# The first head pair's k in a top-32 attention with two gated MLPs: its low parts on VectorE, its last 64 rows first

## The chip, the cores and the metric

One Trainium2 chip, one of its cores. TensorE (PE in the profile; PEld is its weight load) multiplies, VectorE (DVE), ScalarE (ACT) and GpSimd (POOL) do the rest, SyncE (SP) issues the DMAs. The metric is the device time of one execution in microseconds, as the median of three runs: 790.08 us (789.1 to 790.63).

## The reference

For two batches of eight heads, 576 rows and 64 columns, attention keeps for each row the 32 largest scores; two MLPs follow on the 1152 rows of 512.

```
scores = scale * q @ k^T
kth    = the 32nd largest score of each row
attn   = exp(scores - max) where scores >= kth, else 0; divided by its sum
x      = attn @ v, heads side by side          # 1152 x 512
h      = x @ w_in ; g = h * tanh(softplus(h)) ; x = g @ w_out
out    = ((x @ w_a) * (x @ w_b)) @ w_out2
```

The inputs are random float32 values. The MLP weights come as float64 bits and are converted on the chip.

## The kernel before

**Tiles.** The 1152 rows of q make nine tiles of 128 (t = 0 to 8; tile J = 4 holds the last 64 rows of both batches). For each tile there are four steps, one for each pair of heads (hp = 0 to 3). A step transposes and scales q (`prep_q`), and in tiles 0 and 4 also prepares the pair's k (`prep_k`, L106 to L128, for batch 0 and batch 1). Then TensorE makes the scores in four pieces of 288 columns (L176), and ScalarE copies each from PSUM to the tile s2 (L178). VectorE searches the 32 largest: four rounds of MAX8 (L192) with three of MATCH_REPLACE8 (L195) between, for both heads (`largest`). `weighted_sum` (L205) makes the exponentials, transposes them (L227) and multiplies by v (L234).

**High and low parts.** Products that decide which scores are largest are made of two parts: a rounded high part (a cast on ScalarE) and a low part, the remainder (a subtraction). In `prep_k`, `km` holds both parts of the first 512 rows of k for two heads and `kn` those of the last 64 rows. L116 casts, L117 subtracts. The engine of the subtraction comes from `KSUB = (0, 1)`: GpSimd in batch 0, VectorE in batch 1. TensorE then transposes `km` (L122) and `kn` (L125), head by head, and ScalarE copies the results into `kks` (L127), the operand of the scores.

**Weights.** `convert_` (L283) takes 68 tiles of 128x512 from float64 to float32: L293, L294 and L297 on ScalarE, L295 on VectorE, L298 and L299 on GpSimd. It loads them at L288 and stores the result at L306. `weight_` loads them again (L325) and splits them where wanted (L332 to L335).

**MLPs.** Three blocks of tiles (0 to 2, 3 to 5, 6 to 8) go through `gated` and `bilinear`. `product` is L362, `add_product` L369. In `gated` the chain for one slice of columns is: min (L404) on VectorE, four activations on ScalarE, a product (L409) on VectorE, then `gate_parts` (L376, L377), which casts gh on ScalarE and subtracts gl on GpSimd or VectorE. At a block's end y is copied (L417), transposed (L351) and split into yh (ScalarE, L344) and yl (VectorE, L346); `bilinear` multiplies both.

**What sets the order.** Attention and MLP work is written as streams that `together` interleaves. A scheduler then lists the instructions of each engine by priority and by the times that it assumes; each engine works through its list in order. So a small change near the start can move instructions far behind it. PSUM tiles named bank have three buffers, and ks, kr, km and kn have one each.

Of the kernel before, what the change touches and what calls it, by code (L numbers as in the profile page):

```python
# [9 lines left out]
F32 = mybir.dt.float32  # L10
# [22 lines left out]
KSUB = (0, 1)  # L33
# [18 lines left out]
def topk_attention_mlps(ctx: ExitStack, tc: tile.TileContext, q, k, v, w, out):  # L52
# [6 lines left out]
    nc = tc.nc  # L59
    B, H, S, D = q.shape  # L60
# [5 lines left out]
    SM = J * P  # L66
# [21 lines left out]
    def bank(name, n=512):  # L88
        return ps.tile([P, n], F32, name=name, tag="bank", padded_shape=[P, 512])
# [16 lines left out]
    def prep_k(b, hp):  # L106
        ks = wp.tile([P, 2, J, D], F32, name="ks", bufs=BUFS[4])
        kr = wp.tile([R, 2, D], F32, name="kr", bufs=BUFS[4])
        for s in range(2):
            nc.sync.dma_start(ks[:, s], k[b, 2 * hp + s, 0:SM, :].rearrange("(p j) d -> p j d", j=J))  # L110
        nc.sync.dma_start(kr, k[b, 2 * hp:2 * hp + 2, SM:S, :].rearrange("h p d -> p h d"))
        km = wp.tile([P, 2, J, 2, D], F32R, name="km", bufs=BUFS[4])
        kn = wp.tile([R, 2, 2, D], F32R, name="kn", bufs=BUFS[4])
        for z, raw in ((km, ks), (kn, kr)):
            high, low = (z[..., i, :] for i in range(2))
            nc.scalar.copy(high, raw)  # L116
            (nc.gpsimd, nc.vector)[KSUB[b]].tensor_sub(low, raw, high.bitcast(F32))  # L117
        for s in range(2):
            kk = kks[:, (b * H + 2 * hp + s) % (H + 2), :]
            pk = bank("pk")  # L120
            for j in range(J):
                nc.tensor.transpose(pk[:, j * P:(j + 1) * P], km[:, s, j].rearrange("p z d -> p (z d)").bitcast(F32),  # L122
                                    ident)
            pr = bank("pr", R)
            nc.tensor.transpose(pr, kn[:, s].rearrange("p z d -> p (z d)").bitcast(F32), ident[:R, :R])  # L125
            for src, o, n in ((pk, s * R, SM), (pr, SM * (1 - s), R)):
                nc.scalar.copy(kk[:, o:o + n], src)  # L127
            KK[b, 2 * hp + s] = kk  # L128
# [34 lines left out]
    def scores_(t, hp):  # L163
        if hp == 0:
            load_q(t)
        made = prep_q(t, hp)
        if t in (0, J):
            prep_k(t // J, hp)
        s2 = att.tile([P, 2, S], F32, name="s2", bufs=ABUF[0])
        for s in range(2):  # L170
            h = 2 * hp + s
            parts = [(qq, KK[b, h]) for b, qh, ql in made for qq in (qh, ql)]
            for a in range(2):
                psc = bank("psc", HS)
                for n, (qq, kk) in enumerate(parts):
                    nc.tensor.matmul(psc, qq[:, s, :], kk[:, a * HS:(a + 1) * HS],  # L176
                                     start=(n == 0), stop=(n == len(parts) - 1))
                nc.scalar.copy(s2[:, s, a * HS:(a + 1) * HS], psc)  # L178
        return s2
# [338 lines left out]
```

## Time and profile before

| | |
|---|---|
| median of three runs | 790.08 us |
| the profiled execution | 790.78 us |
| its span, first to last instruction | 789.0 us |
| PE busy | 690.1 us (87%) |
| DVE busy | 571.1 us (72%) |
| ACT busy | 550.8 us (70%) |
| POOL busy | 466.0 us (59%) |

The profile comes from one execution. Busy shares over the span mix stages that have different limits, so the work is read stage by stage. 1.78 us of the profiled execution lie outside the span. Starts are counted from the span's start; an idle time in brackets stands behind the instruction that it came before, with what ended it.

### The profile page before, as it was taken

The numbers are of one execution on the slowest core, as the hardware profiler recorded it, in microseconds if no ns is written. First come the engines' busy times: TensorE is split into PE (matmuls) and PEld (weight loads), VectorE is DVE, ScalarE is ACT, GpSimd is POOL, SyncE is SP. The second block draws the span as 40 slices with busy tenths as digits, with TensorE's granted clock in tenths as the row PEclk, the third lists the DMA queues.
The fourth block names the chain that finished last, engine by engine and source line by source line (L and its number), as shares of the span: only waits on it lengthen the run. The fifth ranks groups of instructions, "written<-read, shape, count | busy, mean of one in ns | idle before, by whom it ended". The sixth has DMA issues, their size and how long they took to land. (4 is left out here: it accounts for less than half of the span.)

```text
span 789.0 us, 12393 instructions
## 1 busy us (share of the span) xinstructions
PE 690.1 (87%) x3988; PEld 572.0 (72%) x3988; DVE 571.1 (72%) x1152; ACT 550.8 (70%) x1262; POOL 466.0 (59%) x390
## 2 busy tenths in 40 slices
PE   3565657789977988999999999988999999989997
PEld 2444535556664757889897888867979999969996
DVE  3999999976798789986679998998601276523331
ACT  5889888888997996666668998976524275553232
POOL 6756566676775751456554465552648767665661
PEclk9987667799997998999999999997999999999999
DMA  8987665889989973134334234221403454433411
GB/s 244 288 272 251 209 204 182 225 256 304 354 282 325 342 232 111 54 95 133 94 90 129 78 90 112 80 68 55 134 15 108 119 173 125 131 105 107 125 51 40
DMA packets 79537, 126.12 MB, mean 160 GB/s; under 512 B 27504, under 2 KB 31600, under 8 KB 79472
## 3 DMA queue, kind: packets, MB, share of 16 engines
q1 hardware_dynamic: 79472, 125.33, 52.3%
q8 instruction: 31, 0.51, 0.3%
q14 instruction: 34, 0.28, 0.1%
HBM read 105.12 MB, written 20.19 MB: 159 GB/s over the span
## 5 line engine op out<-in xcount | busy, mean ns | idle before, releaser
L335 POOL TENSOR_TENSOR whl<-raw,whl 128x512 fp32r<-128x512 f32 x164 | 215.3, 1321 | 161.5 <-ACT whl L334 126.6
L192 DVE MAX8 m<-wk 128x8 f32<-128x576 f32 x216 | 158.5, 749 | 1.1
L362 PE MATMUL ph<-yh,whl 128*128 128x384 f32 x576 | 154.6, 340 | 0.7 <-ACT yh L344 0.7
L298 POOL TENSOR_TENSOR w<-w,w 128x512 int32<-128x512 int32 x68 | 89.0, 1309 | 77.8 <-DVE w L295 40.5
L362 PEld LDWEIGHTS ph<-yh,whl 128*128 128x128 f32 x576 | 105.6, 190 | 4.0 <-ACT yh L344 1.6
L195 DVE MATCH_REPLACE8 wk<-m,wk 128x576 f32<-128x576 f32 x144 | 106.4, 741 | 0.0
L362 PE MATMUL ph<-yl,whl 128*128 128x384 f32 x288 | 98.4, 342 | 0.1
L299 POOL TENSOR_TENSOR w<-w,w 128x512 f32<-128x512 f32 x68 | 89.7, 1322 | 7.0 <-ACT w L297 2.2
L234 PE MATMUL px<-et,v 128*64 128x128 f32 (+1 forms) x800 | 76.6, 297 | 17.3 <-ACT et L228 17.0
L334 ACT CAST whl<-raw 128x512 fp32r<-128x512 f32 x113 | 69.3, 622 | 28.8 <-PE ph L362 16.2
L234 PEld LDWEIGHTS px<-et,v 128*64 128x64 f32 x800 | 53.1, 151 | 40.1 <-ACT et L228 26.8
L377 POOL TENSOR_TENSOR gl<-m,gh 128x384 fp32r<-128x384 f32 x52 | 55.5, 1067 | 42.9 <-ACT gh L376 12.1
L362 PE MATMUL ph<-xh,whl 128*128 128x384 f32 x256 | 71.6, 340 | 0.7 <-DVE m L409 0.7
L192 DVE MAX8 m<-s 128x8 f32<-128x576 f32 x72 | 53.9, 751 | 25.2 <-ACT s L178 24.7
L176 PE MATMUL psc<-kks,qh 128*128 128x288 f32 x160 | 57.2, 377 | 13.8 <-ACT kks L127 7.9
L434 DVE TENSOR_TENSOR m<-ph,e 128x384 f32<-128x384 f32 x36 | 19.9, 554 | 67.9 <-PE ph L362 54.9
L376 ACT CAST gh<-m 128x384 fp32r<-128x384 f32 x68 | 34.8, 511 | 48.8 <-DVE m L434 27.6
L227 PE MATMUL pe<-ident,e 128*128 128x128 f32 x324 | 55.7, 305 | 14.7 <-ACT e L220 7.4
L176 PE MATMUL psc<-kks,ql 128*128 128x288 f32 x160 | 51.4, 352 | 11.5 <-DVE ql L155 11.2
L178 ACT COPY s<-psc 128x288 f32<-128x288 f32 x144 | 52.0, 402 | 13.2 <-PE psc L176 12.4
L293 ACT ACTIVATE w<-w 128x512 f32<-128x512 f32 x68 | 46.5, 684 | 20.3 <-DMA w<-in_w_dram 13.5
L228 ACT COPY et<-pe 128x384 f32<-128x384 f32 x108 | 50.3, 487 | 14.6 <-PE pe L227 14.5
(90 smaller groups left out, 1520.3 us busy)
## 6 DMA issues: line engine op xcount, KB each, us to landing
raw<-ws SPq DMA_DIRECT2D x229, 256.0 KB, 2.8
w<-in_w_dram SPq DMA_DIRECT2D x68, 512.0 KB, 4.8
ws<-w SPq DMA_DIRECT2D x68, 256.0 KB, 4.5
qr<-in_q_dram SPq DMA_DIRECT2D x16, 256.0 KB, 4.2
ks<-in_k_dram SPq DMA_DIRECT2D x16, 128.0 KB, 4.3
v<-in_v_dram SPq DMA_DIRECT2D x16, 128.0 KB, 3.9
out_dram<-o SPq DMA_DIRECT2D x8, 256.0 KB, 3.0
qr<-in_q_dram SPq DMA_DIRECT2D x4, 128.0 KB, 8.1
```

What stands on the lines that cost most here:

```text
L176: nc.tensor.matmul(psc, qq[:, s, :], kk[:, a * HS:(a + 1) * HS], start=(n == 0), stop=(n == len(parts) - 1))
L178: nc.scalar.copy(s2[:, s, a * HS:(a + 1) * HS], psc)
L192: nc.vector.max(m8[:, s, got], src[:, s, :])
L195: nc.vector.match_replace(wk[:, s, :], m8[:, s, got], src[:, s, :], NEG)
L227: nc.tensor.transpose(pe[:, i, :], ef[:, n * P:(n + 1) * P], ident)
L234: nc.tensor.matmul(px[s * D:(s + 1) * D, o:o + n], vt[b][:, 2 * hp + s, j, :] if j < J else v4[b][:, hp, s, :], et[:, i if j < J else J, o ...
L298: nc.gpsimd.tensor_tensor(wi, wi, count, op=ALU.add)
L299: nc.gpsimd.tensor_mul(wf, wf, highf)
L334: nc.scalar.copy(wh, raw)
L335: sub().tensor_sub(wl, raw, wh.bitcast(F32))
L362: nc.tensor.matmul(ph, a, x, start=(i == 0), stop=(i == len(mm) - 1))
L377: sub().tensor_sub(gl, g, gh.bitcast(F32))
```

## The change

In `prep_k` the load of `kr` (the last 64 rows of k) is issued ahead of the two loads of `ks`, and the pair (`kn`, `kr`) is cast and subtracted ahead of (`km`, `ks`). This holds for all eight head pairs. For hp = 0 the subtraction is given to VectorE whatever `KSUB` says; since `KSUB` names VectorE for batch 1 already, that moves two instructions, both in batch 0.

```diff
     def prep_k(b, hp):
         ks = wp.tile([P, 2, J, D], F32, name="ks", bufs=BUFS[4])
         kr = wp.tile([R, 2, D], F32, name="kr", bufs=BUFS[4])
+        nc.sync.dma_start(kr, k[b, 2 * hp:2 * hp + 2, SM:S, :].rearrange("h p d -> p h d"))
         for s in range(2):
             nc.sync.dma_start(ks[:, s], k[b, 2 * hp + s, 0:SM, :].rearrange("(p j) d -> p j d", j=J))
-        nc.sync.dma_start(kr, k[b, 2 * hp:2 * hp + 2, SM:S, :].rearrange("h p d -> p h d"))
         km = wp.tile([P, 2, J, 2, D], F32R, name="km", bufs=BUFS[4])
         kn = wp.tile([R, 2, 2, D], F32R, name="kn", bufs=BUFS[4])
-        for z, raw in ((km, ks), (kn, kr)):
+        for z, raw in ((kn, kr), (km, ks)):
             high, low = (z[..., i, :] for i in range(2))
             nc.scalar.copy(high, raw)
-            (nc.gpsimd, nc.vector)[KSUB[b]].tensor_sub(low, raw, high.bitcast(F32))
+            (nc.vector if hp == 0 else (nc.gpsimd, nc.vector)[KSUB[b]]).tensor_sub(low, raw, high.bitcast(F32))
```

The scheduler's lists change from there on, up to about where attention ends. ScalarE's list near the start, as a piece of the difference (- before, + now); s2_132 is the first pair's tile of scores, km_161 and kn_162 belong to the second pair:

```order
+L178 COPY s2_132<-psc_133 128x288
+L116 CAST kn_162<-kr_157 64x2x64
+L178 COPY s2_132<-psc_137 128x288
 L297 ACTIVATE w64_295<-w64_295 128x512
-L178 COPY s2_132<-psc_133 128x288
+L178 COPY s2_132<-psc_141 128x288
 L116 CAST km_161<-ks_156 128x8x64
-L178 COPY s2_132<-psc_137 128x288
-L178 COPY s2_132<-psc_141 128x288
-L116 CAST kn_162<-kr_157 64x2x64
 L178 COPY s2_132<-psc_145 128x288
```

The first two copies of scores now stand ahead of one activation of the weight conversion, and the first pair's kn cast, which is not in this piece, moved to the head of the list, ahead of the scaling of q.

TensorE's list where block 1 ends (tiles 3 to 5), before; pq and psc are the scores of tile 8, third pair, and gh_5793 and gl_5794 are the parts of the last slice of `gated`:

```order
L369 MATMUL acc<-whl,gh_5793 128x512 x6
L234 MATMUL px<-et,v_2954 64x128 x5
L234 MATMUL px<-et,v_2955 64x128 x2
L144 MATMUL pq<-ident,qr 128x128 x2
L369 MATMUL acc<-whl,gl_5794 128x512 x3
L176 MATMUL psc<-kks,qh 128x288 x2
L176 MATMUL psc<-kks,ql 128x288 x2
L176 MATMUL psc<-kks,qh 128x288
L176 MATMUL psc<-kks,ql 128x288
L176 MATMUL psc<-kks,qh 128x288
L176 MATMUL psc<-kks,ql 128x288
L351 MATMUL pt<-ident,y 128x128 x12
```

And the same place now (gh_5612 and gh_5688 are two slices before the last):

```order
L144 MATMUL pq<-ident,qr 128x128 x2
L369 MATMUL acc<-whl,gh_5612 128x512 x6
L369 MATMUL acc<-whl,gl_5613 128x512 x3
L176 MATMUL psc<-kks,qh 128x288
L369 MATMUL acc<-whl,gh_5688 128x512 x6
L176 MATMUL psc<-kks,qh 128x288
L176 MATMUL psc<-kks,ql 128x288 x2
L176 MATMUL psc<-kks,qh 128x288
L176 MATMUL psc<-kks,ql 128x288
L369 MATMUL acc<-whl,gl_5689 128x512 x3
L176 MATMUL psc<-kks,qh 128x288
L176 MATMUL psc<-kks,ql 128x288
```

Between the transposes of q and the scores' second half there now stand products of the MLP; the last slice's (gh_5793, gl_5794) follow the piece shown, straight ahead of the transposes of y.

VectorE's list at the same block end, before; 6301 is the search of tile 8, third pair, and yl_4529 the low part of block 1's y:

```order
L192 MAX m_6301<-s_5817 128x8 x2
L195 MATCH_REPLACE wk<-m_6301,s_5817 128x576 x2
L346 TENSOR_TENSOR yl_4529<-pt,yh_4528 128x4x128
L192 MAX m_6301<-wk 128x8 x2
L346 TENSOR_TENSOR yl_4529<-pt,yh_4528 128x4x128
L195 MATCH_REPLACE wk<-m_6301,wk 128x576
L346 TENSOR_TENSOR yl_4529<-pt,yh_4528 128x4x128
```

And now:

```order
L192 MAX m_6301<-s_5817 128x8
L195 MATCH_REPLACE wk<-m_6301,s_5817 128x576 x2
L192 MAX m_6301<-wk 128x8 x2
L195 MATCH_REPLACE wk<-m_6301,wk 128x576 x2
L192 MAX m_6301<-wk 128x8
L346 TENSOR_TENSOR yl_4529<-pt,yh_4528 128x4x128
L192 MAX m_6301<-wk 128x8
L195 MATCH_REPLACE wk<-m_6301,wk 128x576
L346 TENSOR_TENSOR yl_4529<-pt,yh_4528 128x4x128 x2
```

More of the search stands ahead of the first and of the third yl than before.

## Rows read from the trace of the kernel before

**Rows 1.** Stretches: PE, PEld, DVE, ACT, POOL busy; then clock, DMA share, GB/s.

```profile
0.00:16.22 16.22, 6.50 (x22) 4.41 (x22) 3.85 (x6) 9.93 (x21) 8.68 (x15) 1.00 0.83 238
25.00:150.00 125.00, 78.78 (x422) 58.49 (x420) 123.02 (x262) 107.05 (x255) 80.61 (x63) 0.77 0.74 227
150.00:312.50 162.50, 140.57 (x779) 99.16 (x777) 131.98 (x268) 144.87 (x323) 102.56 (x93) 0.91 0.86 280
412.00:525.00 113.00, 109.87 (x707) 92.67 (x705) 108.29 (x227) 100.05 (x250) 61.89 (x52) 1.00 0.34 94
525.00:541.00 16.00, 11.48 (x73) 8.52 (x71) 15.83 (x34) 11.61 (x29) 4.99 (x4) 0.75 0.17 50
575.00:789.00 214.00, 205.39 (x1070) 184.40 (x1068) 77.38 (x135) 86.81 (x170) 129.33 (x102) 0.99 0.35 101
```

**Rows 2.** The waits view, TensorE, 0 to 25 us: total, times, longest.

```profile
PE pk L122 <- POOL km L117: 5.7, 2, 3.4
...
PE pr L125 <- POOL kn L117: 1.8, 1, 1.8
```

**Rows 3.** The timeline of the first pair: start, us, engine, line, operation, idle before.

```profile
1.85 1.52 SPq L110 DMA_DIRECT2D ks<-in_k_dram  x2
...
3.88 0.75 SPq L111 DMA_DIRECT2D kr<-in_k_dram  x1
...
7.09 1.26 POOL L117 TENSOR_TENSOR km<-ks,km 128x512 fp32r<-128x512 f32 x1 [4.89 <-ACT km L116]
...
8.27 0.67 ACT L293 ACTIVATE w<-w 128x512 f32<-128x512 f32 x1 [1.27 <-DMA w<-in_w_dram]
...
10.84 0.45 POOL L117 TENSOR_TENSOR kn<-kr,kn 64x128 fp32r<-64x128 f32 x1
...
14.41 0.67 ACT L297 ACTIVATE w<-w 128x512 f32<-128x512 f32 x1
...
14.98 0.38 ACT L178 COPY s<-psc 128x288 f32<-128x288 f32 x1
...
15.26 0.62 ACT L116 CAST km<-ks 128x512 fp32r<-128x512 f32 x1
...
15.78 0.70 ACT L178 COPY s<-psc 128x288 f32<-128x288 f32 x2
...
16.22 1.54 DVE L192 MAX8 m<-s 128x8 f32<-128x576 f32 x2 [1.67 <-ACT s L178]
...
16.56 0.40 ACT L178 COPY s<-psc 128x288 f32<-128x288 f32 x1
```

**Rows 4.** All of VectorE's L117: count, ns min/median/max, first and last start.

```profile
L117 DVE TENSOR_TENSOR km<-ks,km x4: 681/822/1235, 54.6 to 301.9; 128x512 fp32r<-128x512 f32 x4
L117 DVE TENSOR_TENSOR kn<-kr,kn x4: 233/270/280, 55.5 to 303.4; 64x128 fp32r<-64x128 f32 x4
```

**Rows 5.** The timeline where a subtraction on VectorE meets GpSimd.

```profile
268.43 1.29 POOL L299 TENSOR_TENSOR w<-w,w 128x512 f32<-128x512 f32 x1
...
269.03 1.24 DVE L117 TENSOR_TENSOR km<-ks,km 128x512 fp32r<-128x512 f32 x1 [1.38 <-PE acc L369]
```

**Rows 6.** The timeline at the end of block 1.

```profile
519.58 0.54 DVE L404 TENSOR_SCALAR e<-ph 128x384 f32<-128x384 f32 x1
...
527.04 1.65 PE L369 MATMUL acc<-whl,gh 128*128 128x512 f32 x6
...
529.83 0.95 PE L369 MATMUL acc<-whl,gl 128*128 128x512 f32 x3
...
530.39 1.41 DVE L192 MAX8 m<-wk 128x8 f32<-128x576 f32 x2
...
533.85 0.85 PE L176 MATMUL psc<-kks,ql 128*128 128x288 f32 x2 [2.77 <-DVE ql L155]
...
538.25 0.68 DVE L346 TENSOR_TENSOR yl<-pt,yh 128x512 fp32r<-128x512 f32 x1
...
541.50 0.68 DVE L346 TENSOR_TENSOR yl<-pt,yh 128x512 fp32r<-128x512 f32 x1
```

## Prediction

> **What bounds the kernel now.** I read the busy time by stretch first, since no engine bounds the whole span [rows 1]. Up to 16.22 us no search runs: VectorE is busy for 3.85 us of it, and its list waits for the first scores. From 25 to 150 us VectorE is busy for 123.02 of 125 us, so the search of the 32 largest sets the pace and everything else fits beside it. From 150 to 312.5 us nothing is full: ScalarE 144.87, TensorE 140.57, VectorE 131.98 of 162.5 us, with the DMA engines at 0.86. From 412 to 525 us TensorE (109.87 of 113) and VectorE (108.29) are both nearly full. From 525 to 541 us VectorE is full (15.83 of 16) and TensorE, with 11.48 us, waits for it. After 575 us TensorE is nearly full to the end. What moves VectorE's start therefore has a way to the end: the search moves, the MLPs start earlier, and TensorE's idle time shrinks. Where two engines are nearly full, only the order of their lists decides what is left of it.
>
> Then I read the waits of the first 25 us. TensorE waits 5.7 us in two waits for km and 1.8 us in one for kn, both from GpSimd [rows 2]. The timeline of the first pair shows why kn is late: its subtraction starts at 10.84 us, behind the weight conversion in GpSimd's list, while km's started at 7.09 us [rows 3]. It also shows who ends last: the first MAX8 starts at 16.22 us, released by ScalarE's copies of the scores, not by k [rows 3].
>
> **The change part by part.** *Two subtractions leave GpSimd and come to VectorE.* Only the first pair of batch 0 moves; the other hp = 0 case was on VectorE already. GpSimd loses 1.26 + 0.45 = 1.7 us [rows 3]. VectorE gains two instructions of kinds that it already runs four times each, 0.68 to 1.24 us for km and 0.23 to 0.28 us for kn [rows 4]. They fall into the first 16.22 us, where VectorE has over 12 us free [rows 1], so they cost nothing on the path; without that cover they would cost 0.9 to 1.5 us. For the duration I take 0.68 us: the long case at 269.03 us ran while GpSimd's L299 was running from 268.43 us [rows 5], and once km's subtraction has left GpSimd, that list has nothing to do there until w's conversion.
>
> The Trainium skill says of this in "SBUF — State Buffer", section "SBUF: two separate sides", that VectorE and GpSimd share one pair of ports, that an operation of VectorE with two SBUF inputs and one of GpSimd that reads SBUF exclude each other, and that the loser blocks for the whole instruction. The trace agrees: 1.24 us beside GpSimd against a minimum of 0.68 us [rows 4, 5]. By that rule a collision here would add 0.56 us to km's low part; without one nothing is added, and neither is seen in the sum, for the reason that follows.
>
> *kr goes ahead of ks.* The issue of kr takes 0.75 us [rows 3]. It now stands ahead of the two issues of ks and of the first load of w, so these leave up to 0.75 us later, and everything behind them leaves as before. With that, VectorE's km subtraction starts between 7.1 us (GpSimd's start before) and 7.85 us and ends between 7.8 and 9.1 us, against 7.09 + 1.26 = 8.35 us before. So km itself gains little or loses a little. What is gained is kn: it is ready before km, and TensorE's 1.8 us of waiting for it goes [rows 2].
>
> *What is late next is ScalarE's list.* From 8.27 us on, when the first weights land, it works through conversions and copies almost without a pause until the scores come [rows 3]. TensorE's 1.8 us are mostly hidden behind it. So I count in ScalarE's list. Two things leave the part ahead of the first copy of scores: the kn cast, 0.2 us of the list, which moves to its head (two copies of 0.28 us and one such cast lie between 15.78 and 16.56 us, so 0.78 - 0.56), and one conversion, which starts at 14.41 us and holds the list until 14.98 us, 0.57 us [rows 3]. The first copy comes at 14.98 - 0.57 - 0.2 = 14.2 us. The second follows after a copy (14.98 to 15.26 us, 0.28) and a kn cast (0.2), where a copy and a km cast stood (0.80): 14.7 us, done at 15.1 us. The first MAX8 so starts at 15.1 us, 1.1 us earlier. The second head's scores gain only the 0.2 us, since the same conversion and km cast now stand in between: the last copy starts at 16.56 - 0.2 = 16.4 us and is done at 16.8 us. VectorE does one MATCH_REPLACE8 in between, and its three operations are done at 16.8 + 0.7 = 17.5 us. Before, the two MAX8 ended at 16.22 + 1.54 = 17.76 us and a third operation of about 0.7 us ended at 18.4 us. The search is then 0.9 us ahead.
>
> The bounds of this: if the first weights land the full 0.75 us later, ScalarE starts its run that much later, and 0.1 us is left. At most it is the 1.8 us that TensorE waited for kn. I take 0.9 us, because kr is only 32 KB in front of 256 KB of ks and 512 KB of weights: what the weights wait for is the transfers, which go on from 2 us, more than the issue. For the second pair, GpSimd's 1.7 us come out of its list ahead of that pair's km, so its scores come earlier by more than the 0.9 us and the search isn't held up. In pairs 1 to 3 of batch 0 and in batch 1 the order of kr and ks alone changes; VectorE is full there [rows 1], and it costs nothing as long as the scores come as early as now.
>
> *The lists are sorted anew.* This is the unknown, because it reaches from 25 us to about 580 us. I weigh it at the one place where TensorE visibly waits for VectorE between 412 and 575 us. Before, TensorE ends block 1 with all MLP products done and then waits 2.77 us for the low part of q before tile 8's scores [rows 6]; from 525 to 541 us it idles 16 - 11.48 = 4.5 us [rows 1]. Now products of two earlier slices stand among these scores and cover that wait. But the last slice's products come straight ahead of y's transposes, and their own chain is long. From L404 at 519.58 us to the product with gh at 527.04 us it took 7.5 us, and to that with gl at 529.83 us 10.25 us [rows 6]. After the last ph, TensorE's list now has two slices of 9 products, 8 score products and the rest of one px. Six products with gh at 1.65 us and three with gl at 0.95 us are 2.6 us a slice as the rows print them [rows 6], less where they overlap; two slices and some 1.5 us for the rest make 5 to 6.7 us of cover. So TensorE waits 0.8 to 2.5 us for gh, and then for gl, which came 2.8 us after gh while the six gh products take 1.65 us, another 1.1 us. Together 1.9 to 3.6 us: about the 2.8 us removed. One wait takes the place of the other, and I put this term at 0. Its ends are -4.5 us (TensorE's idle time there goes altogether) and +2.8 us (below).
>
> *Sum.* 790.78 us for the profiled execution, -0.9 for the start, 0 for the new order: 789.9 us. The profiled execution is 0.7 us above the median of the runs shown, 790.08 us; against that median the forecast is **789.2 us**.
>
> **The rivals.** *A, the forecast:* 0.9 us earlier, the new order about even; by the bounds at the start and a us of disorder, 787.6 to 790.8 us.
>
> *B, the new order fills TensorE's gap.* For it speaks that TensorE and VectorE are both at 96% or more from 412 to 525 us, so that better mixing pays directly, and that at half speed the clock also suffers from the gap: 0.75 granted from 525 to 541 us [rows 1]. Against it speaks the chain of the last slice. If the chain is covered, 790.08 - 0.9 - 4.5 = 784.7 us.
>
> *C, slower: VectorE reaches block 1's yl later.* Its list now has eleven operations of tile 8's third pair ahead of the third yl where there were seven. Four of them at 0.7 us (two took 1.41 us) are 2.8 us [rows 6]. TensorE's yl products need all three yl. VectorE is full up to there [rows 1], so the four can't hide unless it loses idle time elsewhere: 113 - 108.29 = 4.7 us of it lie between 412 and 525 us [rows 1]. The point from which it decides: if the new order recovers less than 1.9 us of that (2.8 - 0.9), the kernel is slower. With none recovered the third yl moves from 541.5 us [rows 6] by 2.8 - 0.9 = 1.9 us, and the time is 790.08 + 1.9 = 792.0 us, or 792.8 us if the start gives only 0.1.
>
> *D, the change at the start does nothing:* ScalarE's list and the landing of the weights hide it all, or the mixed stretch from 150 to 312.5 us swallows it behind the DMA engines (0.86 busy) and ScalarE. 790.1 us. For it speaks that the first MAX8 was released by ScalarE; against it, that two items really leave ScalarE's list ahead of the scores.
>
> **How the numbers follow.** A 0.38, B 0.25, C 0.26, D 0.11. A measurement of this kernel tells about 0.2% from no change, which is 1.6 us: faster is below 788.5 us, slower above 791.7 us. A spans the first bound: 0.13 faster, 0.25 the same. B is faster; C is slower. D gives 0.09 the same and 0.01 to each side. Together 0.39 faster, 0.34 the same, 0.27 slower. The range goes from B's 784.7 us to C's upper end with a little beyond it, 784.6 to 793.0 us.
>
> **What would show it.** In the profile of the changed kernel: kn's subtraction done before km's, both on VectorE before 9.2 us; no wait of TensorE's L125 for GpSimd; the first MAX8 near 15.1 us and the third operation of the search done near 17.5 us; VectorE about 0.9 us ahead through 150 us; the third yl between 538 and 543 us; TensorE's idle time from 525 to 541 us now in front of the last products or gone. It would be wrong if the first weights land 0.75 us later, so that the first MAX8 starts after 15.8 us, or if the stretch from 150 to 412 us, which I count as unchanged though its lists change too, gains or loses more than a few us of idle time.

## The result and the profile after

| | median | runs | ratio to the kernel before (95%) |
|---|---|---|---|
| before | 790.36 us | 4 | |
| changed | 795.52 us | 4 | 1.0068 [1.0045, 1.0092] |

The change makes the kernel about 5 us slower. The forecast was 789.2 us, 784.6 to 793.0, so the time lies outside the range. The profiled span went from 789.0 to 795.3 us.

The head of the kernel came out as worked out. The timeline of the changed kernel's first pair, to be held against [rows 3] (start, us, engine, line, operation, idle time before and its releaser):

```profile
1.85 0.99 SPq L109 DMA_DIRECT2D kr<-in_k_dram  x1
2.88 1.06 SPq L111 DMA_DIRECT2D ks<-in_k_dram  x2
...
5.96 0.28 DVE L117 TENSOR_TENSOR kn<-kr,kn 64x128 fp32r<-64x128 f32 x1 [5.09 <-ACT kn L116]
7.05 0.69 DVE L117 TENSOR_TENSOR km<-ks,km 128x512 fp32r<-128x512 f32 x1
7.80 1.11 PE L122 MATMUL pk<-ident,km 128*128 128x128 f32 x4 [1.71 <-DVE km L117]
8.41 0.67 ACT L293 ACTIVATE w<-w 128x512 f32<-128x512 f32 x1 [1.40 <-DMA w<-in_w_dram]
8.84 0.37 PE L125 MATMUL pr<-ident,kn 64*128 64x64 f32 x1
...
15.01 0.76 DVE L192 MAX8 m<-s 128x8 f32<-128x576 f32 x1 [0.60 <-ACT s L178]
16.67 0.76 DVE L192 MAX8 m<-s 128x8 f32<-128x576 f32 x1
```

Both subtractions are on VectorE and done at 7.74 us, kn's first; the first weights are converted from 8.41 us instead of 8.27; L125 no longer waits for kn; the first MAX8 starts at 15.01 us (forecast 15.1, before 16.22) and the third operation of the search ends at 16.67 + 0.76 = 17.43 us (forecast 17.5).

The loss shows in the stretches, the same as in [rows 1] (PE, PEld, DVE, ACT, POOL busy; clock, DMA share, GB/s), of the changed kernel:

```profile
25.00:150.00 125.00, 79.69 (x418) 59.76 (x417) 123.94 (x264) 108.98 (x257) 81.11 (x63) 0.75 0.73 227
150.00:312.50 162.50, 134.62 (x706) 93.73 (x707) 124.74 (x247) 137.18 (x300) 101.36 (x89) 0.90 0.87 278
...
525.00:541.00 16.00, 15.08 (x101) 12.37 (x99) 16.00 (x34) 14.45 (x36) 11.41 (x10) 1.00 0.25 67
```

Between 150 and 312.5 us VectorE does 124.74 us of work where it did 131.98, ScalarE 137.18 for 144.87 and TensorE 134.62 for 140.57, while DMA share and GB/s are as before. So each of the three has 6 to 8 us of work less behind it by 312.5 us, and the rate of the transfers is the same, 278 for 280 GB/s.

A milestone narrows it: x of tile 2 (L250). It is the attention result times prs, the reciprocals of the rows' sums, and the tile's MLP starts from it. It stood at 227.86 us before; in the changed kernel it is 8.5 us later:

```profile
236.33 0.66 DVE L250 TENSOR_TENSOR x<-xr,prs 128x512 f32<-128x512 f32 x1
```

The way there shows first at the search of tile 2's last (fourth) pair of heads. VectorE's timeline of the kernel before; the MAX8 opens the search of that pair's first head:

```profile
159.89 0.74 DVE L192 MAX8 m<-s 128x8 f32<-128x576 f32 x1
160.56 0.43 DVE L295 TENSOR_SCALAR w<-w 128x512 int32<-128x512 int32 x1
...
163.78 0.43 DVE L295 TENSOR_SCALAR w<-w 128x512 int32<-128x512 int32 x1
...
166.92 0.41 DVE L295 TENSOR_SCALAR w<-w 128x512 int32<-128x512 int32 x1
```

and of the changed kernel:

```profile
161.16 0.69 DVE L409 SCALAR_TENSOR_TENSOR m<-m,ph 128x512 f32<-128x512 f32 x1 [1.95 <-ACT m L408]
163.25 0.43 DVE L295 TENSOR_SCALAR w<-w 128x512 int32<-128x512 int32 x1 [1.40 <-ACT w L293]
166.70 0.43 DVE L295 TENSOR_SCALAR w<-w 128x512 int32<-128x512 int32 x1 [3.02 <-ACT w L293]
...
167.79 0.76 DVE L192 MAX8 m<-s 128x8 f32<-128x576 f32 x1
```

The weight conversions (L295) come at about the same times, 163.25 for 163.78 and 166.70 for 166.92 us. But this search, which ran between them before, now stands behind two of them in VectorE's list and starts 7.9 us later, while VectorE idles 1.95, 1.40 and 3.02 us. VectorE's list is not the whole cause, for the scores themselves come later. TensorE makes them and ScalarE copies them (L178), before:

```profile
153.53 0.61 PE L176 MATMUL psc<-kks,qh 128*128 128x288 f32 x1 [0.62 <-ACT qh L154]
...
158.94 1.01 ACT L178 COPY s<-psc 128x288 f32<-128x288 f32 x3
```

and in the changed kernel:

```profile
156.35 4.45 PE L369 MATMUL acc<-w,m 128*128 128x512 f32 x8
160.64 2.75 PE L362 MATMUL ph<-xf,raw 128*128 128x256 f32 x12
163.05 0.48 PE L176 MATMUL psc<-kks,qh 128*128 128x288 f32 x1
...
165.93 0.68 ACT L293 ACTIVATE w<-w 128x512 f32<-128x512 f32 x1 [0.83 <-DMA w<-in_w_dram]
...
167.07 0.99 ACT L178 COPY s<-psc 128x288 f32<-128x288 f32 x3
```

TensorE starts these scores 9.5 us later, behind 20 products of the MLP that followed them before, and ScalarE copies them behind one more conversion that waited for its load. So the order of three engines' lists holds this search back.

The waits of VectorE from 140 to 236 us say the same. In front of conversions it idles 15.0 us before and 15.2 in the changed kernel. What grew is its idle time in front of other work, from 3.1 to 8.5 us (total, times, longest), before:

```profile
DVE m L192 <- ACT s L178: 2.1, 2, 1.4
...
DVE e L212 <- ACT e L198: 0.5, 1, 0.5
DVE m L409 <- ACT m L408: 0.5, 1, 0.5
```

and in the changed kernel:

```profile
DVE m L409 <- ACT m L408: 2.5, 3, 2.0
DVE rs L243 <- ACT e L220: 2.4, 1, 2.4
DVE e L212 <- ACT e L198: 2.3, 1, 2.3
...
DVE m L192 <- ACT s L178: 1.3, 3, 0.5
```

All of these are waits for ScalarE, which has the conversions' other steps in its own list.

### The profile page after: what moved, and what is told of

Same layout as the page of the kernel before. It is cut to its first block, busy times and chain, and to the rows that moved or that the text cites. A ratio compares the mean times of both kernels' runs of the same rounds, so it can differ in the third digit from the quotient of the medians.

```text
span 795.3 us, 12384 instructions
## 1 busy us (share of the span) xinstructions
PE 689.4 (87%) x3988; PEld 572.7 (72%) x3988; DVE 572.4 (72%) x1154; ACT 552.8 (70%) x1262; POOL 465.8 (59%) x388
## 5 line engine op out<-in xcount | busy, mean ns | idle before, releaser
L299 POOL TENSOR_TENSOR w<-w,w 128x512 f32<-128x512 f32 x68 | 91.1, 1341 | 7.8 <-ACT w L297 3.5
L234 PEld LDWEIGHTS px<-et,v 128*64 128x64 f32 x800 | 54.8, 154 | 40.2 <-ACT et L228 27.0
L176 PE MATMUL psc<-kks,qh 128*128 128x288 f32 x160 | 55.4, 369 | 16.9 <-ACT qh L154 8.7
L227 PE MATMUL pe<-ident,e 128*128 128x128 f32 x324 | 53.7, 299 | 14.9 <-ACT e L220 9.0
L178 ACT COPY s<-psc 128x288 f32<-128x288 f32 x144 | 52.3, 401 | 10.2 <-PE psc L176 9.1
L369 PE MATMUL po<-whl,gh 128*128 128x512 f32 x216 | 59.4, 397 | 0.0
```

What stands on the lines that cost most here:

```text
L227: nc.tensor.transpose(pe[:, i, :], ef[:, n * P:(n + 1) * P], ident)
L234: nc.tensor.matmul(px[s * D:(s + 1) * D, o:o + n], vt[b][:, 2 * hp + s, j, :] if j < J else v4[b][:, hp, s, :], et[:, i if j < J else J, o ...
L299: nc.gpsimd.tensor_mul(wf, wf, highf)
L369: nc.tensor.matmul(acc[i], z[:, i * P:(i + 1) * P], a, start=(first and m == 0), stop=(last and m == len(mm) - 1))
```

## The experiments

**The theories.** *List theory:* the edits gain about 1 us at the head, and the lists that the scheduler sorted anew lose it and more between 140 and 236 us, where the search shares VectorE's in-order list with conversions that wait for weights. *Edit theory:* the subtractions on VectorE or the other load order cost the time themselves. *Any-order theory:* each other order costs some us, spread over the program.

To tell them apart I pinned each engine's list. Every pinned kernel has this at the end of the kernel function, which only fixes the order within an engine and adds no instruction; LISTS holds five lists, one for each engine:

```diff
+    real = [i for i in nc.cur_bb.bb.instructions if type(i).__name__ not in ("BassTilePoolBoundary", "InstRegisterMove")]
+    after = mybir.DependencyInfo(mybir.DependencyClass.NoSync, mybir.DependencyReason.DATA)
+    for seq in listed():
+        for a, b in zip(seq, seq[1:]):
+            tc.add_manual_dep(real[b], real[a].name, after, reason="order")
```

**The edits without the new lists, and the new lists without the edits.** head18 is the changed code; its LISTS are its own up to 18 us and from there those of the kernel before. tail25 is the code before; its LISTS are its own up to 25 us and from there those of the changed kernel.

> The changed code with both edits, but each engine's list pinned: the changed kernel's own order for what starts before 18 us of its profile, and from there the order that the kernel before had. List theory (the loss is made by the re-sorted lists between 140 and 236 us, and the edits gain about 1 us at the head): 788 to 790 us beside about 790.3 of before, 0.9 to 2 us faster at best; prs of tile 2 back at about 221 to 223 us. Edit theory (the two edits themselves cost the time, by two subtractions on VectorE or by weights that arrive later): about 795 us, as in the changed kernel, since both edits are in. Any-order theory (any other order than the one found costs some us): 790 to 795, no place to be named.

Measured: 788.55 us, ratio 0.9975 [0.9962, 0.9987].

> The code of the kernel before without either edit, its lists pinned: its own order for what starts before 25 us, from there the changed kernel's order. List theory: slower than before by what the changed kernel lost and the gain of the head that is missing here, 796 to 797.5 us; x of tile 2 at about 236 to 237 us. Edit theory: about 790, as before, since neither edit is in.

Measured: 795.97 us, ratio 1.0073 [1.0041, 1.0105]; x of tile 2 at 235.0 us. The edits alone gain 2.0 us [1.0, 3.0]; the lists alone lose as much as the whole change did. The edit theory is out. In head18 prs of tile 2 came at 220.2 us and its x at 226.9 us; in the changed kernel they come at 230.9 and 236.3. No run pinned a kernel's own order and changed nothing else, but tail25, pinned, agrees within its interval with the changed kernel, which is sorted freely (1.0068).

**The two halves, sorted freely.**

```diff
-            (nc.gpsimd, nc.vector)[KSUB[b]].tensor_sub(low, raw, high.bitcast(F32))
+            (nc.vector if hp == 0 else (nc.gpsimd, nc.vector)[KSUB[b]]).tensor_sub(low, raw, high.bitcast(F32))
```

This is "subs"; "first" is the rest of the change without it.

> Only one half of the change: VectorE makes k's low parts for the first head pair, the loads and casts stay in the order of before; the lists are sorted anew by the scheduler for this code. Edit theory: if the two subtractions on VectorE cost, 793 to 795. List theory: the time is whatever this sort gives, and the place where it departs from before is not the head; within 785 to 797. If the sort falls as in the kernel before from 140 us on, 789 to 790.

Measured: 805.55 us, ratio 1.0201 [1.0175, 1.0227].

> Only the other half: the last 64 rows of k are loaded and split first, GpSimd makes the low parts as before. Edit theory with the load order as the cause: 793 to 796. List theory: whatever this sort gives, 785 to 797, with the departure from before to be found at the place where another list stands.

Measured: 794.93 us, ratio 1.0046 [1.0025, 1.0066]. Half of the change costs 15 us and the whole 5, so the time does not follow from what the edits add. By itself subs would have spoken for the edit theory; only beside head18, which has the same two subtractions and is faster than before, is it read rightly.

**Where in the lists.** head140 and head240 are spliced as head18, at 140 and at 240 us. allwin and win330 keep the changed kernel's lists except for one stretch, 135 to 250 and 135 to 330 us, in which the order of the kernel before stands. VectorE's list of win330 (+) against the changed kernel's (-), where the search of tile 2's last pair starts (m_1657 on s_1437):

```diff
+L192 MAX m_1657<-s_1437 128x8
+L295 TENSOR_SCALAR w<-w 128x512
+L195 MATCH_REPLACE wk<-m_1657,s_1437 128x576
 L409 SCALAR_TENSOR_TENSOR m_1368<-m_1368,ph 128x512
-L295 TENSOR_SCALAR w<-w 128x512 x2
-L404 TENSOR_SCALAR e_1508<-ph 128x512
-L192 MAX m_1657<-s_1437 128x8
-L195 MATCH_REPLACE wk<-m_1657,s_1437 128x576
```

> The changed kernel's order for all that starts before 140 us of its profile, from there the order of the kernel before. List theory: nothing is lost yet, 788 to 790.5 us, as with the splice at 18 us. If the later place of tile 1's reciprocal in VectorE's list (2 us late in the changed kernel) is what costs: 791 to 793.

Measured: 788.3 us, ratio 0.9956 [0.9934, 0.9979].

> The changed kernel's order for all that starts before 240 us of its profile, from there the order of the kernel before. List theory: x of tile 2 late, at about 236 us, and the delay carried to the end, 794 to 798 us. If the loss is made behind 240 us: 789 to 791.

Measured: 796.69 us, ratio 1.006 [1.0035, 1.0085]; x of tile 2 at 237.8 us. So no loss comes from the order up to 140 us, and the order up to 240 us is enough for all of it.

> The changed kernel with its own lists, but on every engine the instructions that start between 135 and 250 us of its profile are put into the order in which the kernel before had them; ahead of and behind that stretch its own order stands. List theory (loss made in this stretch): x of tile 2 back at about 226 to 229 us, and the whole about 787 to 791 us. If the loss were spread over all of the lists (any-order theory): half of it or more stays, 793 to 796.

Measured: 794.61 us, ratio 1.0038 [1.0013, 1.0062]. This missed. x of tile 2 is back at 227.8 us, as expected, and the time is lost right behind it, at the seam that I made. TensorE's timeline of allwin, where pe is a transpose that it makes and et ScalarE's copy of it:

```profile
237.00 0.49 PE L227 MATMUL pe<-ident,e 128*128 128x128 f32 x3
...
250.32 0.70 PE L234 MATMUL px<-et,v 128*64 128x128 f32 x4 [12.02 <-ACT et L228]
```

and ScalarE's:

```profile
239.59 0.67 ACT L293 ACTIVATE w<-w 128x512 f32<-128x512 f32 x1 [1.18 <-DMA w<-in_w_dram]
...
242.11 0.66 ACT L293 ACTIVATE w<-w 128x512 f32<-128x512 f32 x1 [0.75 <-DMA w<-in_w_dram]
...
245.38 0.67 ACT L293 ACTIVATE w<-w 128x512 f32<-128x512 f32 x1 [1.50 <-DMA w<-in_w_dram]
...
248.14 0.66 ACT L293 ACTIVATE w<-w 128x512 f32<-128x512 f32 x1 [0.98 <-DMA w<-in_w_dram]
...
249.81 0.45 ACT L228 COPY et<-pe 128x384 f32<-128x384 f32 x1
```

The splice put four conversions in a row into ScalarE's list ahead of the copy. Each waits for its load, and TensorE, whose transposes were done at 237.5 us, idles 12.02 us until the copy is made. The seam thus made a loss again by the same means, conversions that wait ahead of critical work, and here in ScalarE's list. win330 has its seam behind the last of the many conversions:

> As with the stretch of 135 to 250 us, but the order of the kernel before holds until 330 us of the changed kernel's profile, past the last of the many weight conversions (the DMA share falls from about 0.7 to 0.35 at 320 us); ahead of and behind it the changed kernel's own order. List theory, with the loss of the shorter stretch made at its second seam, where four conversions stood ahead of the search and TensorE idled 12 us: that idle time goes, 785 to 790 us. If the changed kernel's order behind 330 us costs as well: 793 to 796.

Measured: 787.46 us, ratio 0.9962 [0.9946, 0.9977]. It differs from the changed kernel (1.0068) only in the order between 135 and 330 us, and in that its order is pinned; the order there so costs about 8 us. Behind 330 us it has the changed kernel's order and head140 that of before, and their times can't be told apart: what the two orders differ by there is within about 2 us.

**What paces the conversions.**

```diff
-BUFS = (3, 9, 9, 6, 1)
+BUFS = (4, 9, 9, 6, 1)
```

The first number is the count of buffers for raw weights (w64). after_w4 has the changed kernel's lists pinned, before_w4 those of before, head140_w4 those of head140; after4free is the changed code, sorted freely with this number.

> The changed kernel with its lists pinned as they are, and four instead of three buffers for the raw weights as they land. In the lists VectorE's search stands behind conversions that wait for weights. If these wait because a load waits for a free buffer: the waits of VectorE on converted weights between 150 and 236 us (3.0, 3.3, 2.4 us) shrink and 3 to 8 us come back, 788 to 793. If they wait because the transfers themselves fill the DMA engines (share 0.93 in 150 to 240 us): no change, 794 to 797. Edit theory: no change either.

Measured: 785.41 us, ratio 0.9914 [0.989, 0.9938]: 10 us less than the changed kernel with the same lists, or 12 by the two ratios. The longest waits in SyncE's queue from 140 to 236 us (total, times, longest), of the kernel before:

```profile
SPq L288 <- POOL w L299: 48.2, 26, 4.3
```

of the changed kernel:

```profile
SPq L288 <- POOL w L299: 36.3, 20, 2.8
```

and of after_w4:

```profile
SPq L306 <- POOL w L299: 40.6, 24, 3.8
```

L288 is the load of raw weights, L299 GpSimd's last step on a tile, which gives its buffer back. With three buffers a load waits for that step; with four it no longer does, and the queue waits at the store of the converted tile (L306) instead, with the next load already on its way. The kernel before waits for buffers too, and longer, so this wait by itself is not what the new order lost. VectorE's conversions between 140 and 236 us (their busy time and count; clock, DMA share, GB/s), of the changed kernel:

```profile
140.00:236.00 96.00, 14.81 (x27) 0.91 0.91 290
```

and of after_w4:

```profile
140.00:236.00 96.00, 19.90 (x29) 0.92 0.91 312
```

Two more tiles are converted and the rate rises from 290 to 312 GB/s at the same DMA share. VectorE's idle time in front of conversions in this stretch falls from 15.2 to 8.5 us, and x of tile 2 comes at 229.4 us. The Trainium skill says in "Perfetto Trace Analysis", section "Optimization Strategy", that the same gap, repeating for a stretch on the engine that should be saturated, can mean that there isn't enough SBUF or PSUM for the next tile, by the buffer count or the tile sizes. The trace agrees as far as VectorE is that engine: its gaps in front of conversions shrank by 6.7 us with one buffer more.

> The kernel before with its own lists pinned and four buffers for raw weights. If the wait for a buffer costs only where the search stands behind conversions: little, 787 to 791 us. If slow loads cost every order of this kernel: about 780 to 784 us, the same 10 us as in the changed kernel.

Measured: 787.49 us, ratio 0.9946 [0.9925, 0.9966]. The gain is there in both orders, about 4 us in this one against 10 to 12: how much a buffer is worth depends on the order.

> The changed kernel's order up to 140 us, then that of the kernel before, and four buffers for raw weights. If the two gains add: 785 to 787 us or less; if both repair the same loss: 787 to 789, as with three buffers.

Measured: 784.85 us, ratio 0.9913 [0.9889, 0.9937]. It is faster than both kernels, and so is after_w4. With the order of before the fourth buffer gives 3 to 4 us (head140 to head140_w4, before to before_w4) on top of the head's gain; with the changed kernel's order it gives 10 to 12. With four buffers the two orders (0.9913 and 0.9914) can't be told apart, where with three they are about 8 us apart: the new order costs that much only with three buffers.

> The changed kernel with four buffers for raw weights and nothing pinned: the same lists as the pinned one with four buffers would give 785 us; a sort that knows of the fourth buffer may stand anywhere between 780 and 797 us by the any-order theory.

Measured: 803.83 us, ratio 1.0157 [1.0134, 1.0179], above the expected 797. The edit is that of after_w4, but the new sort is 18 us slower: x of tile 2 comes at 225.9 us, and that of tile 3 at 312.96 us, where after_w4 has it at 298.1.

**Whether the conversions' place in VectorE's list is all.** In convlate2 and convlate4 only VectorE's list of the changed kernel is altered: its 24 conversions that start between 150 and 236 us stand two and four search operations later. VectorE's list of convlate2 (+) against the changed kernel's (-) at one place:

```diff
-L295 TENSOR_SCALAR w<-w 128x512 x2
 L404 TENSOR_SCALAR e_1508<-ph 128x512
 L192 MAX m_1657<-s_1437 128x8
 L195 MATCH_REPLACE wk<-m_1657,s_1437 128x576
-L295 TENSOR_SCALAR w<-w 128x512
+L295 TENSOR_SCALAR w<-w 128x512 x3
 L192 MAX m_1657<-wk 128x8
```

> The changed kernel with its lists pinned, except that the 24 weight conversions of VectorE (the shift in L295) that start between 150 and 236 us stand two search operations later in VectorE's list; all other lists as they are. If the conversions' place ahead of the search in VectorE's list makes the loss: x of tile 2 from 236 to about 230 to 233 us, the whole 789 to 793. If the loss comes from the other engines' lists, or if the later conversion gives its buffer back later and delays the next load by as much: 794 to 798.

Measured: 822.84 us, ratio 1.0408 [1.0377, 1.0439].

> The same with four search operations. If the place ahead of the search is the whole cause: 787 to 792. If later conversions hold back the loads (three buffers, each free only when its conversion is done): 796 to 805, slower than with two.

Measured: 822.34 us, ratio 1.0402 [1.0343, 1.046]. Neither reading had this size, and the two can't be told apart, though convlate4 was expected to be the slower. The simple form of the list theory, that the conversions merely stand too early in VectorE's list, is refuted. The search of tile 2's last pair, from which they were moved away, starts only 1.9 us earlier, and now waits for ScalarE's copies of the scores:

```profile
165.86 0.76 DVE L192 MAX8 m<-s 128x8 f32<-128x576 f32 x1 [0.92 <-ACT s L178]
```

The conversions of convlate2 in the same stretch:

```profile
140.00:236.00 96.00, 10.54 (x19) 0.82 0.72 228
```

and its SyncE queue:

```profile
SPq L288 <- POOL w L299: 52.3, 20, 10.4
```

19 conversions instead of 27, 228 GB/s instead of 290, single waits for a buffer up to 10.4 us, and x of tile 2 at 260.7 us. Load, ScalarE, VectorE, GpSimd, free buffer and the next load are a loop with three buffers. A conversion that comes late holds the loop; a search operation that stands behind one waits for the loop. Moving the conversions in VectorE's list alone did not bring back the order of before; the orders that gained time differ in all five lists.

What stays open: which of the displaced operations between 140 and 330 us costs how much of the 8 us. No run moved ScalarE's or TensorE's list alone, and the traces point to these as much as to VectorE's. The search of tile 2's last pair, 7.9 us late for its first head, is not all of it: for the second head it is 2.9 us late (178.75 for 175.89 us), and the tile's sums rs (L243) are 1.6 us late (192.16 for 190.55 us). The rest arises behind that. TensorE's waits for VectorE's product m (L409), from 140 to 240 us, before:

```profile
PE acc L369 <- DVE m L409: 4.0, 2, 3.4
```

and in the changed kernel:

```profile
PE acc L369 <- DVE m L409: 7.9, 2, 5.0
```

One of these is 2.86 us at 219.33 us, where the kernel before has none: ScalarE's activations from L405 to L408 took from 210.46 to 217.93 us, with two conversions and a pair's exponentials between them, where they took from 208.49 to 211.58 us. TensorE then starts prs of tile 2 at 230.94 us, behind eight products that it used to precede (222.61 us). Last, x starts 4.3 us after prs is done, behind search operations and a conversion in VectorE's list and with VectorE busy (3.3 us before).

## Why the prediction was wrong

*The head* was right, in its steps and in its size: 15.01 us against 15.1, 17.43 against 17.5. Costing the subtractions at nothing held: km's took 0.69 us with GpSimd idle, where 0.68 was taken. What the lead is worth at the end is shown by head18, 2.0 us [1.0, 3.0], so my 0.9 is just below the interval and the bound of 1.8 inside it. But in head18's profile the lead of up to 1 us is gone by 94 us, and the 2 us build up between about 195 and 255 us. So I can't say that they are the same time, and that the size came near may be luck.

*"The lists are sorted anew ... I put this term at 0"* is the step that failed, together with the place where I weighed it. I named it the unknown from 25 to about 580 us and then looked only at the end of block 1, "the one place where TensorE visibly waits for VectorE between 412 and 575 us". The stretch from 150 to 412 us I counted as unchanged, and named its change only as what would make me wrong. The runs put the term at about +8 us, all of it from orders between 135 and 330 us (win330), and the order up to 240 us is enough for it (head140, head240). I had read that stretch's rows [rows 1] as "nothing is full" and weighed no wait there. With no engine full, the waits of one engine for another set the time in it, and these grew: VectorE's in front of other work than conversions from 3.1 to 8.5 us, TensorE's for m from 4.0 to 7.9 us.

*At the end of block 1* no run contradicts the zero: with either order behind 330 us the times can't be told apart (787.46 and 788.3 us). Its parts came out too: the waits for gh and gl in place of the wait for q were forecast at 1.9 to 3.6 us and are 0.68 + 1.66 = 2.34 us. (In the working, most of the 1.1 us counted as wait for gl was TensorE's own other work, which ends at 529.71 us, when gl had been ready since 528.90.) TensorE is 15.08 us busy from 525 to 541 us against 11.48, as rival B had it. But that is work displaced: the last products of block 1 with gl came at 543.04 us, where [rows 6] have them at 529.83, and the third yl after 548.4 us instead of at 541.50. The timeline of the changed kernel there:

```profile
539.75 1.63 PE L369 MATMUL acc<-whl,gh 128*128 128x512 f32 x6 [0.68 <-ACT gh L376]
543.04 0.96 PE L369 MATMUL acc<-whl,gl 128*128 128x512 f32 x3 [1.66 <-POOL gl L377]
...
548.42 1.27 DVE L346 TENSOR_TENSOR yl<-pt,yh 128x512 fp32r<-128x512 f32 x2
```

*Rival C* had the sign, with another mechanism: a later yl, but late from tile 2 on and not by four more operations ahead of it. *Rival D's* time, 790.1 us, does not fit head18, though its thought that the mixed stretch may swallow the lead is not refuted, since the lead is gone by 94 us. None of the rivals had a sort that loses time at a place far from the edit; the range's upper end, 793.0, came from C alone. The free sorts of nearly the same work (before, changed, subs, first, after4free) lie between 790 and 806 us, which is the width that such a term needed.

## What to carry to other kernels

Where a scheduler sorts the lists, a small edit is two changes: what it does, and the new sort. Time them apart by pinning the old order behind the edit before you judge the edit. Weigh the new order first where no engine is full and a loop of few buffers (load, convert, free) runs through the same in-order lists as the critical work. There, count on every engine, not only on the one that idles, which instruction of the loop stands ahead of which critical one; try a buffer more with the order held; and do not take a move later in one list for free, since it holds the loop itself.

## What was not expected of the hardware

A DMA share of 0.91 was not a full one: with one more buffer the same stretch moved 312 instead of 290 GB/s at a share of 0.91. And a loop of three buffers was so stiff that moving 24 VectorE instructions, 13.0 us of work in all, by two search operations in one list made the kernel 27 us slower than with the changed kernel's own order.
